# A fused attention and feed-forward kernel on one core: the later q tiles are split earlier, into other SBUF slots

## The chip, the core and the metric

The kernel runs on one core of a Trainium2 chip. Its engines are named as in the profile: PE (TensorE matmul) and PEld (its weight load), DVE (VectorE), ACT (ScalarE), POOL (GpSimd) and SP (SyncE, here only a DMA queue). The metric is device time in microseconds; before the change it is 815.71 us, the median of three runs (815.21 to 815.78). All engines work in order, each on its own list of instructions, and wait for one another by semaphores.

## What is computed

The reference is random-feature attention, followed by two dense blocks on its output `x` (2304 rows, 512 columns). The part that matters here is the attention:

```python
def phi(x):                       # x: (4, 8, 576, 64), omega: (128, 64)
    proj = np.einsum('bhsd,md->bhsm', x, omega)
    h = proj - np.sum(x * x, axis=-1, keepdims=True) / 2.0
    h = h - np.max(h, axis=-1, keepdims=True)
    return np.exp(h) / np.sqrt(m)
q_p, k_p = phi(q * scale), phi(k * scale)
kv  = np.einsum('bhsm,bhsd->bhmd', k_p, v)
num = np.einsum('bhsm,bhmd->bhsd', q_p, kv)
den = np.einsum('bhsm,bhm->bhs', q_p, np.sum(k_p, axis=2))[..., None] + 1e-06
x   = num / den                   # then (x @ w_in -> softplus -> @ w_out)
                                  # and  ((x @ w1) * (x @ w2)) @ w3 @ w_out
```

## The kernel before

Matrices in float32 are multiplied as two float32r parts: `hi` is the operand cast to float32r, `lo` is the operand less `hi`, and a product is three matmuls (hi·hi, hi·lo, lo·hi; helper `mm3`, line 96, all recorded on line 94).

The work runs in phases. The k phase (to about 50 us) computes the features of k and the sums `kv`. The q phase (about 50 to 130 us) goes over 18 tiles of 128 tokens, `for t in range(nt + XLAG)`, line 735. After it come the dense products, which fill the rest of the span.

One step t of the q phase holds, in the order in which it is written: `q_turn` of tile t-2 (8 transposes on PE, line 392, two copies on ACT, line 394); `q_feat` of tile t in two halves (12 matmuls on PE; the maximum over the features on DVE, `nmax`, line 334; 8 exponentials on ACT, line 339); `split_q(t + 2)` and `load_q(t + 4)`; `q_num` of tile t-3 in two halves (32 small matmuls with `kv` on PE, then on DVE `den`, lines 409 and 410, and `xt`, line 413, which reads the PSUM bank out); and `x_turn` of tile t-4 (4 transposes on PE, line 422, a copy `xs` on ACT, line 424, and a store to the DRAM tensor `xd` on SP, line 425). Every PSUM tile is one of 8 banks, and a step takes 7 of them, so a bank is taken again about a step later.

`split_q` (lines 316 to 322) takes a loaded tile `raw[t]` (pool of 4 buffers, `rawq`) and makes its two parts in one of three buffers `qt0` to `qt2` (`QBUF = 3`): a CAST on DVE (line 287), and a subtraction on POOL (line 288):

```python
def split(hi, lo, f, low=None):
    nc.vector.tensor_copy(out=hi, in_=f)
    (low or nc.gpsimd).tensor_tensor(out=lo, in0=f, in1=hi.bitcast(F32), op=ALU.subtract)
```

Since there are three buffers, a tile can be split when the projection of the tile three before it is done. `load_q` (line 311) is a DMA on the SP queue, in order with the stores of `xs`.

When the sixth tile of `x` has been stored, `operands` (line 433) starts: it loads `xq` from `xd`, and makes sums `s` (line 447) and parts `xa11h`, `xa11l` and so on (lines 454 and 457) for the first dense product. These are pumped one by one from a list, `queue`, by `step(JOB_Q[...])`, and go to slots of the pool `X0` (28 slots, opened at t = 1 on the space of the k phase). `free["X0"]` counts the slots at build time, so that an operation whose slots are not free stays in the list. The operands of one chunk take 14 slots.

The framework orders the instructions of each engine from this program by priority and its own estimate of when operands are there; the order on an engine is then fixed.

Of the kernel before, what the change touches and what calls it, by code (L numbers as in the profile page):

```python
# [20 lines left out]
FR = mybir.dt.float32r  # L21
# [19 lines left out]
HALF = 64  # L41
PRE = 1
QBUF = 3
KBUF = 3
QLAG = 1
N = 384
# [23 lines left out]
def body(ctx: ExitStack, tc: tile.TileContext, q, k, k_rest, v, v_rest, om_t, w_in, w_out, w12, w3, wo, out):  # L70
# [10 lines left out]
    def ps():  # L81
        return ps_.tile([128, 512], F32, tag="ps", name="ps")
# [10 lines left out]
    def matmul(o, a, b, start, stop, **kw):  # L93
        nc.tensor.matmul(out=o, lhsT=a, rhs=b, start=start, stop=stop, **kw)  # L94

    def mm3(o, ahi, alo, bhi, blo, first, last, **kw):
        matmul(o, ahi, bhi, first, False, **kw)
        matmul(o, ahi, blo, False, False, **kw)
        matmul(o, alo, bhi, False, last, **kw)
# [11 lines left out]
    free = {"J": 8, "X0": 28, "X1": 14}  # L111
# [127 lines left out]
    def step(rate):  # L239
        due[0] += rate  # L240
        while due[0] > 0:
            if not pump_one():
                due[0] = min(due[0], 2.0)
                break
            due[0] -= 1
# [20 lines left out]
    Q_ = qstack.enter_context(tc.tile_pool(name="Q_", bufs=1))  # L266
# [5 lines left out]
    def pair(name, bufs):  # L272
        n = small.get(name, (None, 1))[1]
        if n:
            small[name] = sm.tile([128, 2, 4], F32, tag=name, bufs=bufs, name=name), 0
        else:
            small[name] = small[name][0], 1
        return small[name][0][:, 1 - bool(n)]

    kt, vt, kps, kpr, kvs, qts, kacc, raw = {}, {}, {}, {}, {}, {}, {}, {}  # L280
    qbuf = []

# [3 lines left out]
# [3 lines that stand above are left out]
# [10 lines left out]
    def split_k(i):  # L299
        if 0 < i < 2 * B:  # L300
            kt[i] = kt[i - KBUF] if i > KBUF else [K_.tile([128, 2, 512], FR, name=f"kt{i}{x}") for x in "hl"]
            n = 128 if i == 1 else 512
# [8 lines left out]
    def load_q(t):  # L311
        if t < NT // 128:
            raw[t] = Q_.tile([128, 512], F32, tag="rawq", bufs=4, name="rawq")
            nc.sync.dma_start(out=raw[t], in_=q[t])

    def split_q(t):
        if t < NT // 128:
            if len(qbuf) < QBUF:
                qbuf.append(Q_.tile([128, 2, 512], FR, name=f"qt{len(qbuf)}"))
            qt = qbuf[t % QBUF]  # L320
            split(qt[:, 0, :], qt[:, 1, :], raw[t])
            qts[t] = qt.rearrange("p x (c t) -> p x c t", c=4)

    def project(lhs):
        pj = ps()
        for p in range(2):
            a = lhs(p)
            if len(a) == 2:
                mm3(pj[:, 256 * p:256 * p + 256], *a, *om_s, True, True)
            else:  # L330
                matmul(pj[:, 256 * p:256 * p + 256], *a, om, True, True)
        pj = pj.rearrange("p (h m) -> p h m", h=4)
        nmax = pair("nmax", 4)
        nc.vector.tensor_reduce(out=nmax, in_=pj, axis=AX.X, op=ALU.max, negate=True)  # L334
        return pj, nmax

    def features(pj, nmax, dst):
        for h in range(4):
            nc.scalar.activation(out=dst[:, h, :], in_=pj[:, h, :], func=AF.Exp, bias=nmax[:, h:h + 1])  # L339
# [3 lines left out]
    def flush(n):  # L343
        while len(waiting) > n:
            waiting.pop(0)()
# [18 lines left out]
    def kv_sum(i):  # L364
        b, g = divmod(i, 2)
        if g == 0:
            kvs[b] = lined(Q_, H * (D + 1), name=f"kv{b}").rearrange("p (h d) -> p h d", h=H)
        acc = ps()[:, 0:4 * (D + 1)].rearrange("p (h d) -> p h d", h=4)
        for h in range(4):
            for t in range(KT):  # L370
                matmul_half(acc[:, h, :], kps[i][:, t, h, :], vt[i][:, t, h, :], h == 0 and t == 0, False)
            r = 2 * (b // 2) + g
            matmul_half(acc[:, h, :], kpr[r][:, h, :], vrest[:, b % 2, r, h, :], False, h == 3)
        nc.scalar.copy(out=kvs[b][:, 4 * g:4 * g + 4, :], in_=acc)
# [2 lines left out]

    def q_feat(u):
        t, g = divmod(u, 2)
        p = project(lambda p: [qts[t][:, x, 2 * g + p, :] for x in range(2)])  # L380

        def exps():
            qp[u] = M_.tile([128, 4, M], F32, tag="m", name="qp")
            features(*p, qp[u])

        waiting.append(exps)
        flush(QLAG)

    def q_turn(u):
        tp = ps()  # L390
        for h in range(4):
            nc.tensor.transpose(tp[:, 128 * h:128 * h + 128], qp[u][:, h, :], ident)  # L392
        qpt[u] = M_.tile([128, 4, 128], F32, tag="m", name="qpt")
        nc.scalar.copy(out=qpt[u], in_=tp.rearrange("p (h t) -> p h t", h=4))

    def q_num(u):
        t, g = divmod(u, 2)
        nm = ps()
        nm = nm[:, 0:4 * (D + 1)].rearrange("p (h d) -> p h d", h=4)
        lo, hi = 128 * t, 128 * t + 128  # L400
        for h in range(4):
            a = lo
            while a < hi:
                b = a // S
                e = min(hi, (b + 1) * S)
                matmul_half(nm[a - lo:e - lo, h, :], qpt[u][:, h, a - lo:e - lo], kvs[b][:, 4 * g + h, :], True, True)
                a = e
        den = pair("den", 3)[:, :, None]
        nc.vector.tensor_scalar(out=den, in0=nm[:, :, D:D + 1], scalar1=1e-6 * M, scalar2=None, op0=ALU.add)
        nc.vector.reciprocal(out=den, in_=den)  # L410
        if g == 0:
            xt[t] = M_.tile([128, H, D], F32, tag="m", name="xt")
        nc.vector.tensor_tensor(  # L413
            out=xt[t][:, 4 * g:4 * g + 4, :], in0=nm[:, :, 0:D],
            in1=den.to_broadcast([128, 4, D]), op=ALU.mult,
        )

    def x_turn(t):
        tp = ps()
        x = xt[t].rearrange("p h d -> p (h d)")  # L420
        for c in range(KD):
            nc.tensor.transpose(tp[:, 128 * c:128 * c + 128], x[:, 128 * c:128 * c + 128], ident)  # L422
        xs = Q_.tile([128, KD, 128], F32, tag="xs", bufs=2, name="xs")
        nc.scalar.copy(out=xs, in_=tp.rearrange("p (c t) -> p c t", c=KD))
        nc.sync.dma_start(out=xd[:, :, 128 * t:128 * t + 128], in_=xs)


    pools, ready = {}, set()

    def xslot(pool, n, dt, name):  # L430
        return pools[pool].tile([128, n], dt, tag="x", name=name)

    def operands(c, src, pool):

# [220 lines left out]
    def evict_down(d, src, n, name):  # L655
        spare_slot = free["X1"] > 0
        if spare_slot:
            free["X1"] -= 1
        o = xslot("X1", n, F32, name) if spare_slot else mt(n, name=name)
        with tc.high_priority(URGENT):  # L660
            if d % 2:
                nc.scalar.copy(out=o, in_=src)
            else:
                nc.vector.tensor_copy(out=o, in_=src)
        return o, spare_slot
# [57 lines left out]
    queue += job_ops(win[1:2])  # L723
    nt = NT // 128
    begun = None

    def fill():
        nonlocal begun
        if begun is None:
            until(lambda: 0 in ready and win[0].done)  # L730
            x = Up1(0, 0, UP_RATES["Up1"][0])
            begun = x, x.begin_parts()
        next(begun[1], None)

    for t in range(nt + XLAG):
        for g in range(2):
            if 0 <= t - TLAG < nt:
                q_turn(2 * (t - TLAG) + g)
        for g in range(2):
            if t < nt:  # L740
                q_feat(2 * t + g)
            else:
                flush(0)
            step(JOB_Q[0 in xo])
        if t < nt:
            split_q(t + 2)
            load_q(t + 4)
        if t == 1:
            kv_sum(2 * B - 1)
            kstack.close()  # L750
            pools["X0"] = ctx.enter_context(tc.tile_pool(name="X0", bufs=28, side="right", reuse_waits="tile"))
        if 0 <= t - NLAG < nt:
            for g in range(2):
                q_num(2 * (t - NLAG) + g)
        if t >= XLAG:
            x_turn(t - XLAG)
            for c in range(2):
                if t - XLAG == 2 * N // 128 * (c + 1) - 1:
                    xo[c], ops = operands(c, xd, "X0")
                    queue += ops  # L760
        if t in FILL:
            fill()
# [9 lines left out]
    for s in range(NW):  # L772
        n = min(WB, NF * 512 - WB * s)
        pool = "X0"
# [414 lines left out]
```

## Time and profile before

| | |
|---|---|
| median of 3 runs | 815.71 us |
| profiled execution | 814.49 us |
| its span | 812.5 us |
| PE busy | 806.4 us (99%) |
| PEld busy | 756.4 us (93%) |
| DVE busy | 596.8 us (73%) |
| ACT busy | 442.3 us (54%) |
| POOL busy | 29.5 us (4%) |
| granted TensorE clock | full in every slice |

The profiled execution took 814.49 us, of which 812.5 are the span of its instructions and 2.0 lie around it. Busy shares are averages over phases with different limits. An instruction that waits inside its engine for a shared resource is shown as busy, so a duration that is longer than that of its like is also to be read as a wait. Durations of neighbours on one engine overlap somewhat: what an instruction costs the engine is the distance from its start to the next one's start.

### The profile page before, as it was taken

The numbers are of one execution on the slowest core, as the hardware profiler recorded it, in microseconds if no ns is written. First come the engines' busy times: TensorE is split into PE (matmuls) and PEld (weight loads), VectorE is DVE, ScalarE is ACT, GpSimd is POOL, SyncE is SP. The second block draws the span as 40 slices with busy tenths as digits, with TensorE's granted clock in tenths as the row PEclk, the third lists the DMA queues.
The fourth block names the chain that finished last, engine by engine and source line by source line (L and its number), as shares of the span: only waits on it lengthen the run. The fifth ranks groups of instructions, "written<-read, shape, count | busy, mean of one in ns | idle before, by whom it ended". The sixth has DMA issues, their size and how long they took to land.

```text
span 812.5 us, 14558 instructions
## 1 busy us (share of the span) xinstructions
PE 806.4 (99%) x5526; PEld 756.4 (93%) x5526; DVE 596.8 (73%) x1011; ACT 442.3 (54%) x863; POOL 29.5 (4%) x32
## 2 busy tenths in 40 slices
PE   9999999999999999999999999999999999999998
PEld 8989989999999998888888889999999998889998
DVE  7998799878755676755469733898988876889861
ACT  6999898557445676645456522422434223674330
POOL 3033210000000000000000000000000000000000
PEclk9999999999999999999999999999999999999999
DMA  9823625656545558688984632365456556353212
GB/s 300 312 88 105 196 84 168 222 198 217 198 145 195 184 193 261 210 260 295 315 296 163 220 111 90 138 218 182 168 200 231 188 174 233 119 168 125 84 53 77
DMA packets 75861, 150.04 MB, mean 185 GB/s; under 512 B 7184, under 2 KB 44688, under 8 KB 75792
## 3 DMA queue, kind: packets, MB, share of 16 engines
q1 hardware_dynamic: 64016, 101.55, 37.6%
q10 hardware_dynamic: 11776, 47.57, 17.1%
q8 instruction: 43, 0.70, 0.4%
q14 instruction: 26, 0.21, 0.1%
HBM read 98.24 MB, written 50.86 MB: 184 GB/s over the span
## 4 chain that ended last, share of the span: by engine, by line
PE 88%; DVE 5%; ACT 4%; DMA 2%; issue 1%; SPq 0%; DVEq 0%; ACTq 0%
PE ps L94 86%; ACT kp L339 2%; DVE nmax L334 1%; PE ps L392 1%; PE ps L422 1%; DMA rawk<-in_k 1%; DMA xq<-xd 1%; DVE s L447 1%; ACT qp L339 1%; DVE xt L413 0%; DMA xd<-xs 0%; DVE qt L287 0%; DVE kt1h L287 0%; ACT f L136 0%; ACT raw L137 0%
## 5 line engine op out<-in xcount | busy, mean ns | idle before, releaser
L94 PE MATMUL ps<-dhi,lo 128*128 128x512 f32 (+1 forms) x320 | 117.7, 368 | 0.0
L94 PE MATMUL ps<-dlo,hi 128*128 128x512 f32 (+1 forms) x320 | 117.7, 368 | 0.0
L94 PE MATMUL ps<-dhi,hi 128*128 128x512 f32 (+1 forms) x320 | 117.5, 368 | 0.0
L623 DVE TENSOR_TENSOR dlo<-dn,dhi 128x512 fp32r<-128x512 f32 (+1 forms) x80 | 50.4, 635 | 49.5 <-ACT dhi L622 27.9
L622 ACT CAST dhi<-dn 128x512 fp32r<-128x512 f32 (+1 forms) x80 | 45.8, 576 | 55.3 <-DVE dlo L623 29.8
L502 DVE TENSOR_TENSOR c<-ps,u 128x384 f32<-128x384 f32 x144 | 71.5, 548 | 0.8
L94 PEld LDWEIGHTS ps<-dlo,hi 128*128 128x128 f32 x320 | 60.3, 189 | 10.1
L94 PEld LDWEIGHTS ps<-dhi,lo 128*128 128x128 f32 x320 | 60.3, 189 | 10.0
L94 PEld LDWEIGHTS ps<-dhi,hi 128*128 128x128 f32 x320 | 60.3, 189 | 9.9
L502 DVE TENSOR_TENSOR u<-ps,p 128x384 f32<-128x384 f32 x48 | 26.7, 555 | 57.9 <-PE ps L94 56.1
L136 ACT ACTIVATE f<-raw,bias 128x1024 f32<-128x1024 int16 (+2 forms) x43 | 46.6, 1091 | 34.0 <-DVE lo L177 8.5
L542 ACT ACTIVATE c<-c 128x384 f32<-128x384 f32 x72 | 34.9, 524 | 46.5 <-DVE c L502 42.9
L140 DVE SCALAR_TENSOR_TENSOR f<-raw,f 128x1024 int32<-128x1024 f32 (+2 forms) x43 | 45.1, 1048 | 19.7 <-ACT raw L137 19.6
L509 ACT COPY p<-ps 128x384 f32<-128x384 f32 x48 | 22.8, 475 | 61.4 <-PE ps L94 45.8
L334 DVE TENSOR_REDUCE nmax<-ps 128x4 f32<-128x512 f32 x72 | 47.0, 680 | 9.0 <-PE ps L94 9.0
L137 ACT ACTIVATE raw<-raw,bias 128x1024 f32<-128x1024 int16 (+2 forms) x43 | 46.4, 1085 | 0.4
L146 DVE SCALAR_TENSOR_TENSOR f<-raw,f 128x1024 int32<-128x1024 int32 (+2 forms) x43 | 45.0, 1046 | 0.6
L339 ACT ACTIVATE qp<-ps,nmax 128x128 f32<-128x128 f32 x144 | 43.9, 578 | 0.0
L339 ACT ACTIVATE kp<-ps,nmax 128x128 f32<-128x128 f32 x128 | 35.4, 483 | 5.8 <-DVE nmax L334 5.8
L94 PE MATMUL ps<-xs2h,thi 128*128 128x384 f32 x96 | 32.3, 336 | 0.0
L94 PE MATMUL ps<-xs1h,thi 128*128 128x384 f32 x96 | 32.3, 336 | 0.0
L94 PE MATMUL ps<-xs2h,tlo 128*128 128x384 f32 x96 | 32.2, 335 | 0.0
(240 smaller groups left out, 2264.6 us busy)
## 6 DMA issues: line engine op xcount, KB each, us to landing
dn<-gd SPq DMA_DIRECT2D x64, 256.0 KB, 4.2
raw<-in_w ACTq DMA_DIRECT2D x16, 1023.8 KB, 6.1
gd<-c SPq DMA_DIRECT2D x80, 192.0 KB, 2.7
pd<-c SPq DMA_DIRECT2D x48, 192.0 KB, 2.3
raw<-in_w_out ACTq DMA_DIRECT2D x10, 767.8 KB, 4.6
raw<-in_w_in ACTq DMA_DIRECT2D x6, 1023.8 KB, 5.0
rawq<-in_q SPq DMA_DIRECT2D x18, 256.0 KB, 2.7
xd<-xs SPq DMA_DIRECT2D x18, 256.0 KB, 2.8
```

What stands on the lines that cost most here:

```text
L94: nc.tensor.matmul(out=o, lhsT=a, rhs=b, start=start, stop=stop, **kw)
L136: nc.scalar.activation(out=self.f, in_=top, func=AF.Relu, scale=TOP, bias=bias[:, 0:1])
L137: nc.scalar.activation(out=self.words(1, F32, 2), in_=top, func=AF.Identity, scale=TOP, bias=bias[:, 1:2])
L140: nc.vector.scalar_tensor_tensor(out=self.f.bitcast(I32), in0=self.words(1, F32, 2), scalar=-2.0 ** 31, in1=self.f, op0=ALU.max, op1=ALU.min)
L146: nc.vector.scalar_tensor_tensor(out=fi, in0=self.words(0, I32, 2), scalar=13, in1=fi, op0=ALU.logical_shift_right, op1=ALU.bitwise_or,)
L334: nc.vector.tensor_reduce(out=nmax, in_=pj, axis=AX.X, op=ALU.max, negate=True)
L339: nc.scalar.activation(out=dst[:, h, :], in_=pj[:, h, :], func=AF.Exp, bias=nmax[:, h:h + 1])
L502: nc.vector.tensor_tensor(out=z, in0=bank, in1=y, op=ALU.add)
L509: nc.scalar.copy(out=p6, in_=b1)
L542: nc.scalar.activation(out=dst, in_=src, func=AF.Softplus)
L622: nc.scalar.copy(out=hi, in_=got[m])
L623: nc.vector.tensor_tensor(out=lo, in0=got.pop(m), in1=hi.bitcast(F32), op=ALU.subtract)
```

## The change

Tiles from the ninth on (`EARLY = 9`, counted from 0) are no longer split into `qt0` to `qt2` but into two slots each of the pool `X0`, which are counted off in `free["X0"]` and given back after the tile's second projection. From step t = 7 on, each step splits two tiles (and loads two) in place of one, so tiles 9 and 10 come in step 7 and tile 17 in step 11. The number of instructions of each kind is the same. `pools` and `xslot` only move up in the file.

```diff
+EARLY = 9
...
     def split_q(t):
         if t < NT // 128:
-            if len(qbuf) < QBUF:
-                qbuf.append(Q_.tile([128, 2, 512], FR, name=f"qt{len(qbuf)}"))
-            qt = qbuf[t % QBUF]
-            split(qt[:, 0, :], qt[:, 1, :], raw[t])
-            qts[t] = qt.rearrange("p x (c t) -> p x c t", c=4)
+            if t < EARLY:
+                if len(qbuf) < QBUF:
+                    qbuf.append(Q_.tile([128, 2, 512], FR, name=f"qt{len(qbuf)}"))
+                qt = [qbuf[t % QBUF][:, x, :] for x in range(2)]
+            else:
+                free["X0"] -= 2
+                qt = [xslot("X0", 512, FR, f"qt{x}") for x in "hl"]
+            split(*qt, raw[t])
+            qts[t] = [x.rearrange("p (c t) -> p c t", c=4) for x in qt]
...
     def q_feat(u):
         t, g = divmod(u, 2)
-        p = project(lambda p: [qts[t][:, x, 2 * g + p, :] for x in range(2)])
+        p = project(lambda p: [x[:, 2 * g + p, :] for x in qts[t]])
+        if g and t >= EARLY:
+            free["X0"] += 2
...
+    ahead = 2
...
-        if t < nt:
-            split_q(t + 2)
-            load_q(t + 4)
+        for _ in range(2 if t >= EARLY - 2 else 1):
+            split_q(ahead)
+            load_q(ahead + 2)
+            ahead += 1
```

The order of the instructions changes on DVE, POOL and SP. On DVE, from the maximum of tile 6's first half to `xt` of tile 3, these rows stood before (`ps_1400` and `ps_1414` are tile 6's two halves, `ps_1431` and `ps_1445` the `kv` products of tile 3, `rawq_1350` is tile 9):

```order
L334 TENSOR_REDUCE nmax_1407<-ps_1400 128x4
L287 CAST qt0_898<-rawq_1350 128x512
L334 TENSOR_REDUCE nmax_1407<-ps_1414 128x4
L409 TENSOR_SCALAR den_1440<-ps_1431 128x4
L409 TENSOR_SCALAR den_1440<-ps_1445 128x4
L410 RECIPROCAL den_1440<-den_1440 128x4 x2
L413 TENSOR_TENSOR xt_1443<-ps_1431,den_1440 128x256
L413 TENSOR_TENSOR xt_1443<-ps_1445,den_1440 128x256
```

At the same place the changed program has these (`rawq_1516`, `rawq_1597`, `rawq_1603` and `rawq_1684` are tiles 12 to 15):

```order
L293 CAST qth_1599<-rawq_1516 128x512
L344 TENSOR_REDUCE nmax_1407<-ps_1400 128x4
L293 CAST qth_1680<-rawq_1597 128x512
L344 TENSOR_REDUCE nmax_1407<-ps_1414 128x4
L421 TENSOR_SCALAR den_1440<-ps_1431 128x4
L293 CAST qth_1686<-rawq_1603 128x512
L422 RECIPROCAL den_1440<-den_1440 128x4
L421 TENSOR_SCALAR den_1440<-ps_1445 128x4
L425 TENSOR_TENSOR xt_1443<-ps_1431,den_1440 128x256
L422 RECIPROCAL den_1440<-den_1440 128x4
L293 CAST qth_1771<-rawq_1684 128x512
L425 TENSOR_TENSOR xt_1443<-ps_1445,den_1440 128x256
```

Three casts now stand ahead of the first `xt` and a fourth ahead of the second, where one stood. The casts of tiles 9, 10 and 11 stand singly in the three steps ahead of this piece, beside those of tiles 7 and 8, and tile 16's stands behind it. On POOL the order of the subtractions is now tile 6, 9, 7, 10, 8, 11 to 17.

Later on DVE, where the sums of the first dense operands begin, this stood before (`rawq_1833` and `rawq_1918` are tiles 15 and 16):

```order
L447 TENSOR_TENSOR s2_1996<-s1_1914,xq_1730 128x768
L287 CAST qt0_898<-rawq_1833 128x512
L409 TENSOR_SCALAR den_2011<-ps_2002 128x4
L409 TENSOR_SCALAR den_2011<-ps_2016 128x4
L410 RECIPROCAL den_2011<-den_2011 128x4
L287 CAST qt1_913<-rawq_1918 128x512
L413 TENSOR_TENSOR xt_2014<-ps_2002,den_2011 128x256
```

In the changed program the only cast in this part of DVE is that of tile 17 (`rawq_1775`), two steps earlier than the piece above, at the first of these sums:

```order
L454 TENSOR_TENSOR s3_1859<-xq_1754 128x768
L293 CAST qth_1861<-rawq_1775 128x512
L422 RECIPROCAL den_1874<-den_1874 128x4
L421 TENSOR_SCALAR den_1874<-ps_1879 128x4
L425 TENSOR_TENSOR xt_1877<-ps_1865,den_1874 128x256
L422 RECIPROCAL den_1874<-den_1874 128x4
L464 TENSOR_TENSOR xa11l_1844<-xq_1754,xa11h_1843 128x768
```

The casts of tiles 15 and 16 have left this part, and tile 17's has moved up to where tile 17's slots are taken from the pool.

## Rows read from the trace of the kernel before

**Rows 1.** Busy time by stretch: us, PE, PEld, DVE, ACT, POOL, clock, DMA share, GB/s.

```profile
65.00:84.00 19.00, 18.82 (x270) 17.51 (x268) 15.43 (x49) 18.91 (x59) 5.50 (x5) 1.00 0.43 131
...
92.00:127.00 35.00, 34.27 (x461) 31.30 (x459) 32.00 (x85) 33.46 (x95) 5.95 (x5) 1.00 0.46 140
```

**Rows 2.** Chain that ended last, in order of time: start us, us, what.

```profile
92.46 5.03 DMA xq<-xd
...
106.84 1.50 DVE qt L287
```

**Rows 3.** Timeline, PE: start us, us, engine, line, operation, count.

```profile
73.47 0.36 PE L94 MATMUL ps<-omh,qt 128*128 128x256 f32 x1
...
77.44 0.36 PE L94 MATMUL ps<-omh,qt 128*128 128x256 f32 x1
...
97.29 0.36 PE L94 MATMUL ps<-omh,qt 128*128 128x256 f32 x1
...
119.21 0.36 PE L94 MATMUL ps<-omh,qt 128*128 128x256 f32 x1
```

**Rows 4.** Timeline, DVE, a step of the middle of the q phase.

```profile
69.26 0.41 DVE L287 CAST qt<-rawq 128x512 fp32r<-128x512 f32 x1
...
74.46 0.69 DVE L334 TENSOR_REDUCE nmax<-ps 128x4 f32<-128x512 f32 x1 [1.12 <-PE ps L94]
75.11 0.43 DVE L287 CAST qt<-rawq 128x512 fp32r<-128x512 f32 x1
75.45 0.68 DVE L334 TENSOR_REDUCE nmax<-ps 128x4 f32<-128x512 f32 x1
76.06 0.37 DVE L409 TENSOR_SCALAR den<-ps 128x4 f32<-128x4 f32 x2
76.35 0.29 DVE L410 RECIPROCAL den<-den 128x4 f32<-128x4 f32 x2
76.62 0.76 DVE L413 TENSOR_TENSOR xt<-ps,den 128x256 f32<-128x256 f32 x2
```

**Rows 5.** Timeline, DVE, its first casts and the late q phase.

```profile
44.67 2.19 DVE L287 CAST qt<-rawq 128x512 fp32r<-128x512 f32 x3
...
105.36 0.95 DVE L447 TENSOR_TENSOR s<-s,xq 128x768 f32<-128x768 f32 x1
106.23 0.42 DVE L287 CAST qt<-rawq 128x512 fp32r<-128x512 f32 x1
...
106.84 1.50 DVE L287 CAST qt<-rawq 128x512 fp32r<-128x512 f32 x1
108.27 0.41 DVE L413 TENSOR_TENSOR xt<-ps,den 128x256 f32<-128x256 f32 x1
...
114.72 2.04 DVE L447 TENSOR_TENSOR s<-xq,s 128x768 f32<-128x768 f32 x1
116.68 0.41 DVE L413 TENSOR_TENSOR xt<-ps,den 128x256 f32<-128x256 f32 x1
```

**Rows 6.** Timeline, POOL.

```profile
75.67 1.28 POOL L288 TENSOR_TENSOR qt<-rawq,qt 128x512 fp32r<-128x512 f32 x1 [2.69 <-DVE qt L287]
...
106.78 1.28 POOL L288 TENSOR_TENSOR qt<-rawq,qt 128x512 fp32r<-128x512 f32 x1 [9.98 <-DVE den L409]
...
114.65 1.29 POOL L288 TENSOR_TENSOR qt<-rawq,qt 128x512 fp32r<-128x512 f32 x1 [4.90 <-PE ps L392]
```

**Rows 7.** Waits of PE over the span: us in total, times, longest.

```profile
PE ps L94 <- DVE xt L413: 0.8, 3, 0.4
```

**Rows 8.** Timeline, ACT.

```profile
90.25 2.20 ACT L339 ACTIVATE qp<-ps,nmax 128x128 f32<-128x128 f32 x8
...
97.52 0.84 ACT L454 CAST xa11h<-xq 128x768 fp32r<-128x768 f32 x1 [1.12 <-DMA xq<-xd]
...
116.32 2.61 ACT L339 ACTIVATE qp<-ps,nmax 128x128 f32<-128x128 f32 x8
```

**Rows 9.** The tile rawq: its loads from issue to landing.

```profile
DMA to landing us min/median/max: 2.4/2.7/7.2
```

More of the change, by code (lines that the diff above doesn't have):

```diff
@@ L278, in pair, with xslot @@
         return small[name][0][:, 1 - bool(n)]
+    pools, ready = {}, set()
+    def xslot(pool, n, dt, name):
+        return pools[pool].tile([128, n], dt, tag="x", name=name)
     kt, vt, kps, kpr, kvs, qts, kacc, raw = {}, {}, {}, {}, {}, {}, {}, {}
@@ L425, in x_turn @@
         nc.sync.dma_start(out=xd[:, :, 128 * t:128 * t + 128], in_=xs)
-    pools, ready = {}, set()
-    def xslot(pool, n, dt, name):
-        return pools[pool].tile([128, n], dt, tag="x", name=name)
     def operands(c, src, pool):
```

## The prediction

> **What bounds the kernel now.** The page gives PE as busy for 99% of the span, so an edit counts by what it does to the moments at which PE has to stand still. I read the busy time by stretch first. In the middle of the q phase, 65 to 84 us, DVE has the most air of the three engines that matter (15.43 us busy of 19.00, ACT 18.91); in the late q phase, 92 to 127 us, DVE has 32.00 and ACT 33.46 of 35.00 [rows 1]. The chain that ended last says the same in another way: it runs on PE through the middle, goes over the loading of `xq` (5.03 us from 92.46), and then along DVE, with one cast of 1.50 us on it [rows 2].
>
> The PE timeline gives the size of it. In the middle a step is 3.97 us long (first projection at 73.47, the next at 77.44), PE's own work without a gap. From the projection at 97.29 to the one at 119.21 lie five steps: 21.92 us, where five of 3.97 would be 19.85. So the late part loses 2.07 us on PE [rows 3]. That is all that early splitting could win there.
>
> DVE in the middle step: idle 1.12 us before the first `nmax`, then `nmax` and one cast 0.34 us apart, the second `nmax` 0.61, two `den` 0.29, two reciprocals 0.27, two `xt` 0.76 [rows 4] (distances from start to start; six such steps, with 1.05 to 1.12 us idle in each). Read on these rows alone, a second cast a step would fit into the idle time three times over.
>
> The row that speaks against it is in the late part. A cast takes 0.42 us at 106.23, but 1.50 at 106.84 [rows 5]. In between, at 106.78, POOL began the subtraction that belongs to the first cast; it ran 1.28 us, to 108.06, and DVE's next instruction started at 108.27 [rows 6, 5]. The same at 114.72: a sum `s` takes 2.04 us, where its like takes 0.95 at 105.36, and a POOL subtraction covers 114.65 to 115.94 [rows 5, 6]. So a DVE instruction that takes all its large operands from SBUF stands still until a running POOL instruction has ended. `nmax`, `den` and `xt`, which read PSUM, pass beside POOL: those of 76.06 to 77.38 run at their usual length under the subtraction of 75.67 to 76.95 [rows 4, 6].
>
> **The change part by part.** No instruction is added or removed. Eighteen casts and eighteen subtractions remain, so what counts is the place.
>
> *The late part, relieved.* The casts of tiles 15 and 16 leave it: 0.33 us and, with its wait, 1.43 (106.84 to 108.27). The cast of tile 17 leaves its old place, 0.34, and with its subtraction goes the wait of `s`, 2.04 - 0.95 = 1.09. Together 3.2 us of DVE. Tile 17's cast comes back at the first sum, with 0.34, and its subtraction now stands in the way of `xa11l`. That takes all it reads from SBUF and is issued about 0.6 us after the cast (reciprocal, `den`, `xt`, reciprocal), while POOL is busy until 0.22 + 1.28 = 1.50 after it, so it waits about 0.8. Net 2.1 us of DVE, about what PE loses there. But the same steps are nearly full on ACT, which the change does not touch: 33.46 of 35.00 us. Of the 1.54 left, 1.12 is the wait for the load of `xq` [rows 8], which stays, since the stores before it follow PE. The eight exponentials of 116.32 take 2.61 us in place of 2.20 [rows 8], 0.41 of hidden waiting. So ACT can come in by 1.54 - 1.12 + 0.41 = 0.8 us at most. The bounds of the gain are 0 and PE's 2.1. I take 0.6, near ACT's limit, since the wait of `xa11l` puts `nmax` later once.
>
> *The middle, loaded.* Ten casts, of tiles 7 to 16, now stand on DVE within some four steps. Each starts a subtraction on POOL, 0.56 us after its own start (75.11, 75.67) [rows 4, 6], that is 0.22 after the cast frees DVE. The next cast, if it comes while that runs, frees DVE 0.21 after POOL's end. From one blocked cast to the next that makes 0.22 + 1.28 + 0.21 = 1.71 us, whatever PSUM work (0.4 to 0.7 us) lies between them. Following the order after the change:
>
> Tile 7's cast stood at 69.26 [rows 4]; tile 9's now stands ahead of it, so 69.60. It frees DVE at 69.94, and POOL runs 70.16 to 71.44. Tile 10's cast comes after one `xt` and a reciprocal, waits, and frees DVE at 71.65. Then `xt` 0.35, two `nmax` 1.21, two `den` 0.29, a reciprocal 0.1: tile 8's cast starts at 73.6 without waiting, and POOL runs 74.16 to 75.44. Tile 11's cast waits and frees DVE at 75.65. From here every cast meets the subtraction of the one before: tile 12 frees DVE at 77.36, tile 13 at 79.07, tile 14 at 80.78. Then come a reciprocal, a `den` and the first `xt` of tile 3, which is done at about 81.3. Before, it was done by 77.0.
>
> PE needs that `xt`. In the built program the second half of tile 7's projection writes the bank that this `xt` reads out, and the trace shows PE waiting for `xt` in just this manner, three times, 0.4 us at the longest [rows 7]. Tile 7's projection begins at 77.44 [rows 3], about 0.5 later by the 0.34 of tile 9's cast and a short wait for the second `xt` of tile 2. Its second half is due 0.8 after that, at 78.7, and gets the bank at 81.3 + 0.1: 2.6 us of standing still, 3.1 with the 0.5 before. Behind it on PE queue everything of that step: `kv` of tile 4, the transposes, tile 8's projection. The casts of tiles 15 and 16 follow at 82.5 and 84.2, under PE work that is now late itself, so they add nothing; from there DVE has no casts, and PE goes on at 3.97 a step.
>
> The loads keep up: tile 12's buffer is free at 71.44, its load lands 2.7 us after issue [rows 9], at some 74.5, and its cast is due at 75.65. The stores of `xs` on the SP queue now stand behind loads that wait for POOL, the second store by some 3 us; each has a step's time before its buffer is needed, so I cost this at nothing. If that cover went, the load of `xq` would slip with them.
>
> The bounds of this term: below, 0, if the banks absorb it. Above, all waits of the seven blocked casts (about 5.6) and the five added casts (1.7), with no idle time to take them: 7.3. I take 3.1.
>
> [...]
>
> *The sum.* 3.1 - 0.6 = 2.5 us on the profiled execution's 814.49 (span 812.5 and 2.0 around it): 817.0. That execution lies 1.2 us under the median of 815.71, so the median is forecast at 818.2. After 127 us PE is dense to the end, and nothing there gives a delay back.
>
> **The rivals.**
>
> *Faster, the late relief decides.* The waits in the middle are taken by DVE's idle time (1.1 us a step) and by the banks, and PE keeps its 3.97. Then PE wins up to the 2.07 of the late part: 813.6. For it: the wait is on DVE, which in the middle is not the bound. Against it: four blocked casts in a row make 6.8 us where a step is 3.97. It decides from the point at which the first `xt` of tile 3 is done before 78.7.
>
> *No measurable change.* Some casts slip in before POOL has begun: the three casts at 44.67 take 2.19 us together [rows 5], 1.2 more than three free ones, so one of them waited and not two. With half the waits the cost is about 1.5, the gain 0.9 as PE comes less late to the late part: 815.71 + 0.6 = 816.3. Against it: only casts that follow one another directly could do so, and in the new order each has `nmax`, `den` or `xt` between.
>
> *Slower still, loads late.* The longest load of a q tile took 7.2 us [rows 9]. If tile 12's did, its cast would wait until 79, some 3.3 us beyond its place: 821.5. Against it: the median is 2.7 and the DMA share of that stretch is 0.43 [rows 1].
>
> That the change doesn't do what it says holds for tile 17 alone, which is costed above.
>
> **How the numbers follow.** Forecast 0.52, loads late 0.08, no measurable change 0.25, faster 0.15. The forecast's own range is 817.4 to 820.0; the whole one reaches down to 814.6, which leaves some 0.1 of the faster case outside, and up to 820.4, with most of the late loads outside. About 0.2%, 1.6 us, is what a measurement of this kernel can tell from no change; by that measure: faster 0.15, same 0.25, slower 0.60.
>
> **What would show it.** In the changed profile: casts of about 1.5 us in the middle, six or more of them, each ending just after a POOL subtraction; POOL with a subtraction every 1.7 us from about 74 to 84 us; one wait of PE for `xt` of 2 to 3 us near 79 to 81; the projections after it about 3 us later than before and again 3.97 apart; in the late part, no cast but tile 17's, and steps of 4.1 to 4.2 us, set by ACT. I am wrong if the casts there keep to 0.43 us, or if they wait and PE's steps stay at 3.97 nonetheless; and wrong in the gain if the late steps fall to 3.97.

## The result, and the profile after

The changed kernel takes 820.12 us (median of 6 runs, 819.13 to 822.37), the kernel before 815.46 beside it (6 runs): the ratio is 1.0055, 95% interval 1.0041 to 1.0070. The forecast was 818.2, slower. The direction and the wait on POOL came as written; the loss is 4.7 us where 2.5 were forecast, so the size was about 2 us short. The time lies 0.1 above the forecast's own range (817.4 to 820.0) and 0.3 inside the end of the whole one (820.4); that it falls inside is in part luck.

The profiled execution of the changed kernel has a span of 817.6 us, 5.1 more than that of before. To see where they lie, I use three marks on each trace: the first projection of tile 2, that of tile 8, and the first load of `dn`, with which the next phase begins. Before, they stand at 58.03, 81.40 and 292.04 us; after, at 58.64, 86.53 and 296.59. The first 0.6 us arise before the change begins, and vary between executions of all kernels here (tile 2 stands anywhere from 58.0 to 60.9). From tile 2 to tile 8 the change costs 4.52 us (27.89 against 23.37), from tile 8 on it gives 0.58 back.

Busy time by stretch, after (columns as in [rows 1]):

```profile
65.00:84.00 19.00, 16.06 (x202) 14.66 (x202) 18.94 (x44) 15.93 (x50) 11.91 (x10) 0.95 0.60 165
...
92.00:127.00 35.00, 34.38 (x489) 32.05 (x488) 30.01 (x82) 33.33 (x99) 1.30 (x1) 1.00 0.40 123
```

In the middle PE has lost 2.8 us and DVE is full, 18.94 of 19.00, where [rows 1] has 15.43. POOL is busy 11.91 in place of 5.50. In the late part DVE and POOL are relieved, as planned. The granted clock is new: 0.95 in the first row, where [rows 1] has 1.00.

The DVE timeline of the middle, after (it answers to [rows 4]):

```profile
70.93 1.36 DVE L293 CAST qth<-rawq 128x512 fp32r<-128x512 f32 x1
...
74.76 1.37 DVE L293 CAST qth<-rawq 128x512 fp32r<-128x512 f32 x1
...
76.39 1.39 DVE L293 CAST qth<-rawq 128x512 fp32r<-128x512 f32 x1
...
78.29 1.12 DVE L293 CAST qth<-rawq 128x512 fp32r<-128x512 f32 x1
...
80.01 1.03 DVE L293 CAST qth<-rawq 128x512 fp32r<-128x512 f32 x1
...
81.23 0.42 DVE L425 TENSOR_TENSOR xt<-ps,den 128x256 f32<-128x256 f32 x1
81.66 1.01 DVE L293 CAST qth<-rawq 128x512 fp32r<-128x512 f32 x1
...
83.53 0.78 DVE L293 CAST qth<-rawq 128x512 fp32r<-128x512 f32 x1
```

And POOL under it:

```profile
74.56 1.29 POOL L294 TENSOR_TENSOR qt<-rawq,qt 128x512 fp32r<-128x512 f32 x1 [0.86 <-PE ps L404]
76.21 1.27 POOL L294 TENSOR_TENSOR qtl<-rawq,qth 128x512 fp32r<-128x512 f32 x1 [0.36 <-DVE qth L293]
...
79.50 1.26 POOL L294 TENSOR_TENSOR qtl<-rawq,qth 128x512 fp32r<-128x512 f32 x1 [0.36 <-DVE qth L293]
```

Read the two together: the subtraction of 74.56 ends at 75.85, the cast of 74.76 at 76.13, and 0.08 later the next subtraction begins. POOL sets the pace, one every 1.62 to 1.65 us. The first `xt` of tile 3 is done at 81.65.

PE at that place, after (the brackets give the idle time before and what ended it):

```profile
78.52 0.36 PE L95 MATMUL ps<-omh,qt 128*128 128x256 f32 x1
...
81.81 0.36 PE L95 MATMUL ps<-omh,qt 128*128 128x256 f32 x1 [2.33 <-DVE den L422]
...
83.15 2.00 PE L95 MATMUL ps<-kv,qpt 128*64 128x65 f32 x32
...
86.53 0.36 PE L95 MATMUL ps<-omh,qt 128*128 128x256 f32 x1
...
88.13 1.15 PE L95 MATMUL ps<-kv,qpt 128*64 128x65 f32 x32
```

Half of tile 7's projection, 2.33 us of standing still, the other half. But the `kv` matmuls behind it take 2.00 us, and the same 32 in the next step 1.15. The windows say why (PE's busy time is the first number behind the length, the granted clock the third from the end):

```profile
79.50:81.80 2.30, 0.00 (x0) 0.02 (x1) 2.24 (x8) 2.30 (x8) 1.94 (x2) 1.00 0.90 250
81.80:83.00 1.20, 1.19 (x6) 1.13 (x6) 1.20 (x3) 0.30 (x2) 0.84 (x2) 0.60 0.86 182
83.00:84.00 1.00, 1.00 (x18) 0.85 (x18) 1.00 (x3) 0.36 (x2) 1.00 (x1) 0.50 0.99 307
...
85.00:86.00 1.00, 1.00 (x11) 0.92 (x8) 0.80 (x5) 0.01 (x1) 0.66 (x1) 0.77 0.00 0
```

After the wait PE is busy all the time, but at a granted clock of 0.50 until about 85.5. From 81.81 to tile 8's projection it needs 4.72 us. Before, tile 7's step is 3.96 us long, and the 0.96 up to 79.48 had been done, so 3.00 were left: 1.72 us are lost behind the wait. Not all of it is the clock: in two of the kernels below that stop at the same place and keep a clock of 1.00, the same piece takes 3.25 us (82.98 to 86.23 in again, 81.07 to 84.32 in one). So 1.47 us go with the low clock, and 0.25 with stopping in the middle of a projection at all.

The granted clock of the whole run shows the loss as well: 0.997 or 0.998 in all six runs of the changed kernel, 0.999 or 1.000 in every run of the kernel before that lists it.

The late part, PE's tile steps and the one cast that is left there, on DVE:

```profile
102.42 0.36 PE L95 MATMUL ps<-omh,qth 128*128 128x256 f32 x1
107.06 0.36 PE L95 MATMUL ps<-omh,qth 128*128 128x256 f32 x1
111.57 0.36 PE L95 MATMUL ps<-omh,qth 128*128 128x256 f32 x1
...
123.52 0.36 PE L95 MATMUL ps<-omh,qth 128*128 128x256 f32 x1
```

```profile
102.99 0.42 DVE L293 CAST qth<-rawq 128x512 fp32r<-128x512 f32 x1
...
104.03 1.57 DVE L464 TENSOR_TENSOR xa11l<-xq,xa11h 128x768 fp32r<-128x768 f32 x1
```

Five steps take 21.10 us in place of the 21.92 of [rows 3]: 0.82 won. Two of the steps are still long (4.64 and 4.51), the ones behind the landing of `xq` and tile 17's cast; `xa11l`, which takes 0.93 where nothing is in its way, waits for that cast's subtraction.

### The profile page after: what moved, and what is told of

Its sections match the earlier page's. It is cut to its first block, busy times and chain, and to the rows that moved or that the text cites. A ratio compares the mean times of both kernels' runs of the same rounds, so it can differ in the third digit from the quotient of the medians.

```text
span 817.6 us, 14555 instructions
## 1 busy us (share of the span) xinstructions
PE 809.0 (99%) x5526; PEld 758.2 (93%) x5526; DVE 602.0 (74%) x1011; ACT 442.9 (54%) x863; POOL 29.8 (4%) x32
## 4 chain that ended last, share of the span: by engine, by line
PE 85%; DVE 7%; ACT 4%; DMA 3%; issue 1%; POOL 0%; SPq 0%; DVEq 0%; ACTq 0%; POOLq 0%
PE ps L95 84%; ACT kp L349 2%; DMA xq<-xd 1%; DMA rawk<-in_k 1%; DVE nmax L344 1%; PE ps L404 1%; DVE qth L293 1%; DVE xt L425 1%; PE ps L434 1%; DVE s L454 1%; ACT qp L349 1%; DVE c L509 0%; DMA xd<-xs 0%; DVE xa11l L464 0%; ACT f L137 0%
```

## The experiments

The theory at this point: the clustered casts wait for POOL (one every 1.62 to 1.65 us), so the first `xt` of tile 3 is late (81.65), so PE waits for its bank (2.33 us), and the idle PE then loses half its clock (0.50). The table sums up what was measured; the last two columns are read from each kernel's trace at the marks above, that is from one execution each. Two kernels were profiled twice (the end of this section): the column up to tile 8 came out within 0.02 us of the first time, the one up to `dn` moved by 1.3 and 2.2. So a microsecond in the last column tells nothing by itself.

| kernel | median, us | ratio to before, 95% interval | tile 2 to tile 8 | tile 2 to `dn` |
|---|---|---|---|---|
| before | 815.46 to 815.97 | 1 | 23.37 | 234.01 |
| after | 820.12 | 1.0055 (1.0041 to 1.0070) | 27.89 | 237.95 |
| nosub | 815.61 | 0.9994 (0.9984 to 1.0004) | 24.14 | 233.06 |
| twice | 819.94 | 1.0056 (1.0044 to 1.0068) | 29.02 | 238.48 |
| again | 819.31 | 1.0044 (1.0027 to 1.0060) | 26.39 | 236.63 |
| one | 818.65 | 1.0038 (1.0026 to 1.0049) | 24.48 | 237.58 |
| spaced6 | 814.90 | 0.9990 (0.9981 to 0.9999) | 23.37 | 232.31 |
| spaced7 | 817.53 | 1.0021 (1.0008 to 1.0035) | 23.37 | 236.86 |
| pin1 | 818.70 | 1.0036 (1.0022 to 1.0049) | 23.36 | 237.06 |

**nosub: the casts without POOL.**

```diff
-                qt = [xslot("X0", 512, FR, f"qt{x}") for x in "hl"]
-            split(*qt, raw[t])
+                hi = xslot("X0", 512, FR, "qth")
+                nc.vector.tensor_copy(out=hi, in_=raw[t])
+                qt = [hi, hi]
+            if t < EARLY:
+                split(*qt, raw[t])
```

> The early splits of tiles 9 to 17 keep their cast on DVE, at the same places, but POOL does no subtraction for them: the high part is used as the low part too, so the numbers of these tiles are left out of the reckoning. Theory (each clustered cast waits for the POOL subtraction of the cast before it, so xt of tile 3 is late, TensorE waits 2.3 us for a PSUM bank, and its clock then falls): the casts take 0.4 to 0.5 us, no TensorE wait above 0.6 us between 65 and 92 us, granted clock 1.00 in every stretch there, the late gain of 0.8 us stays: 814.7 us (814.0 to 815.4). Rival one (DVE simply has more instructions in front of xt, whatever POOL does): a wait of 1 us or more stays and the time is 817.5 to 820. Rival two (the raw q tiles land too late, and the casts wait for them): casts still spaced 1.6 us, 818 to 820.

Measured: 815.61 us. From tile 2's projection to 92 us DVE has the same instructions in the same order as in the changed kernel, and its casts at the disputed place are:

```profile
77.80 0.41 DVE L331 CAST qth<-rawq 128x512 fp32r<-128x512 f32 x1
...
78.73 0.41 DVE L331 CAST qth<-rawq 128x512 fp32r<-128x512 f32 x1
...
79.81 0.43 DVE L331 CAST qth<-rawq 128x512 fp32r<-128x512 f32 x1
80.42 0.42 DVE L428 TENSOR_TENSOR xt<-ps,den 128x256 f32<-128x256 f32 x1
```

The longest wait of PE from 65 to 92 us is 0.4, and the clock is 1.00 in that whole stretch. Of the 4.52 us up to tile 8, 0.77 remain: two casts still take 1.36 and 1.37 behind the subtractions of tiles 7 and 8, which were left in. So neither the casts nor their order cost the time, but POOL under them; both rivals fall. The median is 0.9 above what I expected, 0.2 beyond my range, and the interval holds no change: without the loss, the whole gain of early splitting is within 0.2% too.

**twice: a longer hold of POOL.**

```diff
             split(*qt, raw[t])
+            if t >= EARLY:
+                nc.gpsimd.tensor_tensor(out=qt[1], in0=raw[t], in1=qt[0].bitcast(F32), op=ALU.subtract)
```

> The POOL subtraction of tiles 9 to 17 is done twice over, into the same place. Theory (casts wait for POOL): cast to cast 2.9 us instead of 1.65, xt of tile 3 later by three to four subtractions (3.8 to 5.1 us), TensorE's wait grows from 2.3 to 6 or 7 us, and its clock falls after it as in the changed kernel: 824 to 827 us. Rival one (the order of DVE's own instructions) and rival two (late loads): POOL's length does not matter, 820 us (819.5 to 821).

Measured: 819.94 us, the same as the changed kernel. My expectation failed by 4 us and more, and the one number of the rivals was met. The trace shows that this does not bring them back, though. POOL, then DVE:

```profile
77.75 1.28 POOL L294 TENSOR_TENSOR qtl<-rawq,qth 128x512 fp32r<-128x512 f32 x1 [0.36 <-DVE qth L293]
79.10 1.34 POOL L333 TENSOR_TENSOR qtl<-rawq,qth 128x512 fp32r<-128x512 f32 x1
80.41 1.46 POOL L294 TENSOR_TENSOR qtl<-rawq,qth 128x512 fp32r<-128x512 f32 x1
```

```profile
77.92 1.38 DVE L293 CAST qth<-rawq 128x512 fp32r<-128x512 f32 x1
...
79.83 0.90 DVE L293 CAST qth<-rawq 128x512 fp32r<-128x512 f32 x1
```

The cast of 77.92 ends at 79.30, behind POOL's first subtraction (79.03) and not behind the second, which runs to 80.44. So here a waiting DVE instruction is let in between two POOL instructions, and what it waits for is the one that is running, although POOL has the next one ready: no cast of this stretch takes longer than 1.38 us. It is then POOL that is held up (1.34 and 1.46 us in place of 1.28). I had multiplied by POOL's queue. PE's waits there are 0.85, 0.56 and 1.91 us, and behind the last of them, which ends at 82.90, the clock falls again, the third number from the end:

```profile
84.00:85.00 1.00, 1.00 (x32) 1.00 (x28) 0.23 (x1) 0.73 (x3) 0.92 (x2) 0.75 0.54 129
85.00:86.00 1.00, 1.00 (x8) 0.88 (x7) 0.09 (x1) 0.41 (x2) 1.00 (x1) 0.50 0.35 133
```

Of this kernel's five runs three list a granted clock of 0.997 or 0.998 and two 1.000, so it does not fall each time.

**again: work for the waiting PE.**

```diff
+AGAIN = 11
...
+        if u == AGAIN + 4:
+            turn_again(AGAIN, 16)
         p = project(lambda p: [x[:, 2 * g + p, :] for x in qts[t]])
...
+        if u == AGAIN:
+            again.append(tp)
+        else:
+            nc.scalar.copy(out=qpt[u], in_=tp.rearrange("p (h t) -> p h t", h=4))
+
+    again = []
+
+    def turn_again(u, n):
+        tp, behind = again.pop(), newest[0]
+        for i in range(n):
+            h = i % 4
+            ins = nc.tensor.transpose(tp[:, 128 * h:128 * h + 128], qp[u][:, h, :], ident)
+            tc.add_manual_dep(ins.ins, behind.ins.name, ...)
         nc.scalar.copy(out=qpt[u], in_=tp.rearrange("p (h t) -> p h t", h=4))
```

The number `u` counts half tiles: 11 is tile 5's second half, 15 tile 7's. `newest[0]` is the last matmul written before, and `add_manual_dep` orders the transposes behind it.

> The changed kernel with 16 extra transposes on TensorE (four transposes of tile 5's second half done five times in all, same values into the same place; the ACT copy that reads them comes behind them). They stand exactly where TensorE waits 2.3 us, behind the first half of tile 7's projection, and last about 2.1 us by the 1.04 us that eight of them took. DVE's and POOL's work is unchanged, so the bank comes no earlier. Theory (the waiting TensorE loses its clock, and the slow matmuls afterwards cost 1.7 us): granted clock 1.00 from 80 to 88 us, second half of tile 7's projection 0.8 us instead of 1.3, kv matmuls 1.1 instead of 2.0, time 818.4 us (817.8 to 819.2), less than the changed kernel although it does more. [...] Rival two (ACT or DVE take back whatever TensorE gains): clock full, but 819.7 to 820.5.

Measured: 819.31 us. PE, and the windows of the same place:

```profile
80.48 1.91 PE L422 MATMUL ps<-ident,qp 128*128 128x128 f32 x16
82.98 0.36 PE L98 MATMUL ps<-omh,qt 128*128 128x256 f32 x1 [0.60 <-DVE den L440]
...
83.86 1.15 PE L98 MATMUL ps<-kv,qpt 128*64 128x65 f32 x32
...
86.23 0.36 PE L98 MATMUL ps<-omh,qt 128*128 128x256 f32 x1
```

```profile
81.80:83.00 1.20, 0.60 (x7) 0.40 (x5) 1.14 (x6) 1.20 (x5) 0.84 (x2) 1.00 0.93 258
83.00:84.00 1.00, 1.00 (x10) 0.87 (x12) 1.00 (x2) 0.26 (x1) 0.64 (x2) 1.00 1.03 294
```

The bank comes as late as in the changed kernel (23.14 us behind tile 2's projection, there 23.17), DVE and POOL do what they did, the DMA share is as high (0.93 to 1.03), and sixteen more matmuls run; but the clock stays at 1.00, the `kv` matmuls take 1.15, and tile 8 comes 1.50 us earlier (26.39 against 27.89). So it is the standing still that costs the clock, not the traffic. The expected 1.7 is nearly met there; up to `dn` 1.32 of it are left, since a wait at 106 us takes 0.84 in place of 0.45, and the medians differ by 0.8, less than I had expected. The median lies 0.1 beyond my range, and the two ratios' intervals overlap (1.0027 to 1.0060, 1.0041 to 1.0070), so the times alone do not show the gain. The clock does, and not in one execution only: 0.999 or 1.000 in all six runs of this kernel, 0.997 or 0.998 in all six of the changed one.

**one: the new slots, one split a step.**

```diff
-        for _ in range(2 if t >= EARLY - 2 else 1):
+        for _ in range(1):
```

> One split a step as before, only the slots are the new ones (tiles from the ninth on no longer share three buffers). Theory: fewer casts stand together (tiles 8, 10 and 11), so TensorE's wait is 0 to 1 us and its clock stays at or near 1.00; the last casts are late again, so no late gain: 816.5 us (815.4 to 817.6). Rival (the new slots alone bring the loss, by where they lie or what they wait for): 819 or more.

Measured: 818.65 us, 2 above my expectation, and between my range (up to 817.6) and the rival's 819. The middle is as the theory has it: one wait of 0.45 us, clock 1.00, 1.11 us lost up to tile 8. The other 2.5 are lost in the late part, where the casts of the last tiles stand, and again behind POOL. DVE, then PE:

```profile
105.47 0.41 DVE L293 CAST qth<-rawq 128x512 fp32r<-128x512 f32 x1
...
106.08 1.98 DVE L464 TENSOR_TENSOR xs3l<-s,xs3h 128x768 fp32r<-128x768 f32 x1
107.99 0.41 DVE L425 TENSOR_TENSOR xt<-ps,den 128x256 f32<-128x256 f32 x1
```

```profile
108.45 0.69 PE L95 MATMUL ps<-kv,qpt 128*64 128x65 f32 x16 [1.54 <-DVE xt L425]
```

A subtraction of 0.93 us takes 1.98 behind a cast's POOL work, the `xt` behind it is late, PE waits 1.54 us. After this wait the granted clock stays at 1.00. The time does not rule out the rival, that the new slots as such bring the loss; spaced6 below does, which has the same slots and loses nothing.

**spaced6: the same splits, kept apart.** Two splits a step from step 6, each cast ordered on DVE behind a named instruction.

```diff
+FROM = 6
...
+            if t >= FROM and g == 1:
+                split_next("nmax")
...
                 q_num(2 * (t - NLAG) + g)
+            if t >= FROM:
+                split_next("xt")
```

`split_next` does one split and one load; its cast is ordered behind the last `nmax` or `xt` written before.

> The same splits, as far ahead in the end, two a step from step 6 on, but each cast is ordered on DVE behind a named instruction: one behind the second nmax of a step, one behind the second xt, so that casts stand about 2 us apart and find POOL idle. Theory: casts of 0.4 to 0.6 us, no TensorE wait above 0.6 us between 65 and 92 us, granted clock 1.00, late gain kept: 814.7 us (814.0 to 815.5), under the kernel before. Rival one (any cast added in this stretch delays xt, by its own time and its place): 817 to 819. Rival two (late loads): casts wait for their DMA and hold up what is behind them, 818 or more.

Measured: 814.90 us, ratio 0.9990, interval 0.9981 to 0.9999: the fastest kernel of this study, if by little. DVE in a step:

```profile
82.79 0.61 DVE L296 CAST qth<-rawq 128x512 fp32r<-128x512 f32 x1
83.94 1.41 DVE L349 TENSOR_REDUCE nmax<-ps 128x4 f32<-128x512 f32 x2 [0.53 <-PE ps L96]
85.26 0.42 DVE L296 CAST qth<-rawq 128x512 fp32r<-128x512 f32 x1
86.09 0.76 DVE L430 TENSOR_TENSOR xt<-ps,den 128x256 f32<-128x256 f32 x2
86.77 0.55 DVE L296 CAST qth<-rawq 128x512 fp32r<-128x512 f32 x1
```

Every second cast meets the last 0.3 us of a subtraction and takes 0.55 to 0.61 us in place of 0.42, none more; DVE has idle time again, and tile 8 comes 23.37 us behind tile 2, exactly as before. The casts also come later: seven lie between these two marks, twelve in the changed kernel. But they come two a step, the steps behind tile 8's stay at 3.97 us, and the last cast is done by 95.3 us. So two casts a step cost PE nothing when they stand apart; that the changed kernel's twelve cost their 4.5 us by what POOL does under them, and not by their number, is what nosub shows.

**pin1 and spaced7: what the late part needs.** pin1 leaves out the split behind `nmax`, spaced7 begins the pairs one step later.

> The evenly spaced kernel with one split a step instead of two: from step 6 on the cast is ordered on DVE behind the second xt of its step; the slots are the new ones; no split is more than two steps ahead. Theory: the middle is clean (tile 8's projection 23.4 us behind tile 2's, as before), and in the late part the cast of each step starts a POOL subtraction under the 768 wide subtractions of DVE, which take up to 2.0 us instead of 1.0: nothing is gained late, 815.8 us (815.0 to 817.0). Rival (it was the order of the casts alone, not the distance ahead, that made the evenly spaced kernel faster): 814.9 us or less. Rival two (the new slots or the single split lose by themselves, as in the kernel with one split a step): 818 or more.

> The evenly spaced kernel, with the pairs of splits begun one step later (from step 7, as in the change). Theory: the same as the evenly spaced kernel, no TensorE wait above 0.6 us between 65 and 92 us, casts done before the late part but the last one; 815.0 us (814.2 to 815.8), 0.5 to 1.2 under the kernel before. Rival (its gain was chance, or one place that begins a step earlier): 815.8 or more.

Measured: 818.70 and 817.53 us. Both are clean in the middle (23.36, 23.37), so the theory of the middle held; both lose 2.9 to 3.1 us behind it, which I had not expected. Both times are those of the rivals that I had named, 818 or more for pin1 and 815.8 or more for spaced7; the slots alone can't be the reason, since spaced6 has the same ones. PE in spaced7, what it waited for on DVE, and the clock after:

```profile
102.70 1.15 PE L96 MATMUL ps<-kv,qpt 128*64 128x65 f32 x32 [1.71 <-ACT xs L441]
...
105.86 0.69 PE L439 MATMUL ps<-ident,xt 128*128 128x128 f32 x2 [1.64 <-DVE xt L430]
```

```profile
101.33 0.96 DVE L459 TENSOR_TENSOR s<-xq 128x768 f32<-128x768 f32 x1 [3.27 <-DMA xq<-xd]
102.21 0.42 DVE L296 CAST qth<-rawq 128x512 fp32r<-128x512 f32 x1
...
102.95 1.86 DVE L469 TENSOR_TENSOR xa11l<-xq,xa11h 128x768 fp32r<-128x768 f32 x1
```

```profile
106.00:107.00 1.00, 1.00 (x6) 1.00 (x7) 1.00 (x2) 1.00 (x4) 0.00 (x0) 0.50 0.00 0
```

Two things meet here. One cast, tile 17's, is left to the late part, and `xa11l` waits for its subtraction: 1.86 us. And `xq` landed 6.4 us behind its issue, where it took 5.0 before and 4.3 in spaced6. To see whether that belongs to the kernel, both were profiled once more.

> The evenly spaced kernel begun at step 7, profiled once more. In its first profile the middle was clean, but the first load of xq landed 6.4 us behind its issue (before: 5.0; evenly spaced from step 6: 4.3), DVE and ACT waited 3.3 and 2.9 us for it, and TensorE 1.7 and 1.6 us behind them. If the landing varies from one execution to the next: it lands in 4 to 5.5 us this time, and TensorE waits under 1 us there. If it belongs to this kernel's order of loads: again 6 us or more, and the same waits.

> The evenly spaced kernel begun at step 6, profiled once more. If the landing of xq varies by chance: somewhere between 4 and 6.5 us, and with over 6 the late part loses 2 us or more. If it belongs to the kernel: 4.0 to 4.8 us, DVE waits under 0.8 us for it, and the time from tile 2's projection to the first load of dn is again 232.3 us within 0.4.

Measured (819.55 and 815.74 us, one execution each): `xq` landed in 5.4 us in both, and from tile 2 to `dn` it took 234.71 in spaced7 and 233.56 in spaced6. So the landing varies from one execution to the next by a microsecond, and the time up to `dn` with it, by 1.3 and 2.2 us; neither expectation fits as a whole. In spaced7 a fall of the clock goes with the later landing: in the first profile TensorE waits 1.71 and 1.64 us and the clock falls (0.50 from 106 to 109 us, 0.998 over the run), in the second 0.67 and 1.64 and the run lists 1.000. Four of spaced7's ten runs list a clock of 0.998; their median is 818.7 us, that of the other six, at 1.000, 816.9. At the same landing the two kernels differ by 1.15, and spaced7 has the same wait of 1.64 us for `xt` as in its first profile: the trace puts that part on tile 17's cast. In nosub, where no subtraction follows this cast, `xa11l` takes its 0.93 us. Why `xq` lands later in one execution than in another, and how much of pin1's loss it makes (6.3 us there), stays open.

## Why the prediction was right, and where it was short

- **Casts wait for POOL, about 1.5 us, six or more.** Right: seven, of 0.78 to 1.39 us. The pace was forecast at 1.71 and is 1.62 to 1.65, since POOL begins 0.16 us after a waiting cast has freed DVE (76.05, 76.21) and not 0.22. Shown to be the cause by nosub.
- **First `xt` of tile 3 done at 81.3.** It is done at 81.65, on an execution that runs 0.6 late: 81.0. That a cast of tile 9 came at 66.73 already, three us ahead of its place in my walk through the order, changed nothing, because the pile begins later.
- **One wait of PE, 2.6 us, 0.5 before it.** Measured 2.33 and 0.47. Right.
- **"Behind it on PE queue everything of that step", at its usual length.** This is the step that failed. The sum took PE's work after the wait at the durations of before; it ran at a granted clock of 0.50 up to about 85.5 us, and the term of the middle is 4.5 in place of 3.1: 2.8 as forecast, and 1.7 behind the wait, of which 1.5 are the clock, as again shows. Every row of PE that I had read showed a clock of 1.00, and no wait for `xt` in it was longer than 0.4 us [rows 7]; I had forecast one six times as long, and not asked what PE is like after it.
- **The late gain, 0.6, held down by ACT.** Measured 0.82 over the five steps, 0.58 up to `dn`. The size agrees, but it is that of one execution, where others of one kernel differ by 1.3 to 2.2 us up to `dn`, so this may be luck. The form is not right: I had written even steps of 4.1 to 4.2 us, and there are two of 4.5 to 4.6 behind the landing of `xq` and three of 3.97 to 4.01. The bound from ACT, 0.8, was too low: spaced6 gains 1.70 and 0.45 in its two profiles, nosub 1.72 behind tile 8.
- **"Nothing there gives a delay back."** Right within the start's variation: from `dn` to the end 520.5 us before, 521.0 after.
- **The rivals.** Faster needed the `xt` done before 78.7; it was not. No change needed casts that slip in before POOL; none did. Late loads: the casts kept POOL's pace to the end, so no load held them up in the middle; but the load that varies, that of `xq`, matters more than I gave it.

The trace accounts for 3.9 us between tile 2 and `dn`; the medians differ by 4.7. The rest is within what executions differ by at their start.

## What to carry to other kernels

Before work is moved into an engine's idle time, look at what each moved instruction starts elsewhere: here a DVE cast with a POOL subtraction behind it held the next cast back, so that two of them needed up to 1.65 us between them, not 0.4. Two a step, placed 1.5 to 2.5 us apart, they cost nothing here. When a change makes TensorE wait much longer than it did in the trace of before (here 2.33 us, where no wait for `xt` had been longer than 0.4), do not price the work behind it at the old durations: here the granted clock fell to 0.50 for 3.5 us, and 2.8 us became 4.5, most of the difference by the clock.

## What was not expected of the hardware

TensorE's granted clock fell from 1.00 to 0.50 behind a single wait of 2.33 us (after), behind one of 1.91 (twice, with two shorter ones some microseconds earlier, and in three of five runs only), and behind two of 1.71 and 1.64 with 1.5 us of work between them (spaced7, in the profiled execution); it stayed up behind a single one of 1.54 (one) and behind 0.67 and 1.64 (spaced7's second profile). In after it fell 0.2 us after TensorE was at work again, in twice some 1.6 us after. It was back at 1.00 at 85.5 us (after), TensorE having worked without a gap since 81.81. In again sixteen transposes that nothing needs, in the place of that wait (0.60 us of it were left), kept the clock at 1.00. Why the clock fell behind some of these waits and not behind others, no run shows.

In twice a DVE cast that was blocked by POOL got in as soon as the running POOL instruction had ended, even with another one ready behind it (POOL's ended at 79.03, the cast at 79.30); POOL was the one that then waited (1.34 and 1.46 us in place of 1.28).
